# Three conversion steps of the second expert unit moved behind the third unit's rows, and a store taken out of the scatters' order

## The chip, the cores and the metric

The kernel runs on one core of a Trainium2 chip. The metric is the time of one execution on the device in microseconds (us). Five engines work side by side, each through its own queue in order: TensorE (PE, its weight loads shown apart as PEld), VectorE (DVE), ScalarE (ACT), GpSimd (POOL) and SyncE (SP), which issues nearly all transfers. They wait for one another by semaphores.

## The reference

Three layers follow one another: attention, a mixture of experts with one expert for each token, and a dense pair of layers with an ELU between them.

```python
scores_l = scale * q @ k.T ; scores_l where |pos_i - pos_j| < 16 else -1e9
scores_s = scale * q @ max_of_32(k).T + log(32)
a = softmax(concat(scores_l, scores_s)) ; x = a @ concat(v, mean_of_32(v))
...
expert_idx = argmax(x @ w_gate) ; gate_w = its softmax value      # 8 experts
disp[e, n] = x of the n-th token of expert e, up to capacity 384
y = relu(disp @ w1[e]) @ w2[e] ; out[i] = gate_w[i] * y[its place]
...
h = out @ w_in ; g = h if h > 0 else exp(h) - 1 ; result = g @ w_out
```

There are 2 x 768 = 1536 tokens of 512 values; w1 and w2 are 512x1024 and 1024x512 for each expert, w_in is 512x2048 and w_out 2048x512. w_in and w_out arrive as 64-bit floats.

## The kernel before

**First stage.** Twelve tiles of 128 tokens pass through attention and the gate. The gate of a tile (`gate_1` to `gate_4`) finds its expert and the token's place there; `put` then writes the tile's 128 rows of 514 floats to the DRAM buffer `xdisp` by an indirect transfer that POOL issues (L775). All twelve transfers belong to a group "put" whose members do not wait for one another. Behind the expert regions `xdisp` has 384 spare rows, which SP fills with a constant (`fill`, L904) in the step `n == 21`, two steps before the stage ends. The first unit's rows are read back early (`XROW0`, scaled at L267).

**Second stage.** The experts that got tokens are worked on in units of up to 384 rows, one unit behind the other, behind branches on the number of units (`units`, `unit`). With this input three units run. In each, eight tiles of hidden values are formed (`hidden`, products at L241) and used three tiles later (`second_1`, products at L275). Each float32 operand is split in a rounded part (ACT) and a remainder (DVE): the weights at L233/L234 (`split_a`, names wa..) and L286/L287 (`split_b`, names wb..), hidden values at L1270/L1271 (hh, hl), the unit's rows at L256/L257 (`split_x`, xh, xl). The rows of the third unit are split in its prologue, at the head of `unit(2)`.

**Conversions.** Beside that, DVE turns the 64-bit w_in and w_out into float32, a pair of 128-row blocks at a time, in three steps each (L419, L422, L412, tiles win and wout from raw). `ORDER` gives the sequence of the 16 pairs. The second unit does places 5 to 9 of it and the third unit places 10 to 14, spread over the hidden tiles by `convert_some`. Two raw buffers, `raw0` and `raw1`, take turns; the third step of a pair has SP load the pair after next into the buffer just freed (L378, `conv_next`).

**Third stage.** `group` works through the dense layers in groups of 384 rows (L241 again, and L1383).

Work is put on each engine in the order in which the code is written; no scheduler reorders it. In `unit`, for hidden tile `f`, that order is: finish the last unit's tile, hidden products, the split of the next weights, ReLU and split of the hidden values, `convert_some(j, f)`, `second_1(f - 3)`, `split_b`, and for the second unit at `f == 6` the split of the third unit's first weights (`prologue(2, 0)`).

Of the kernel before, what the change touches and what calls it, by code (L numbers as in the profile page):

```python
# [26 lines left out]
E, F = 8, 1024  # L27
FF = 2048
P = 128
# [9 lines left out]
REG = NT + SLOT  # L39
# [55 lines left out]
def moe_chain_kernel(  # L95
# [14 lines left out]
    nc = tc.nc  # L110
# [3 lines left out]
    xdisp = dram.tile([E * REG + SLOT, ROW], F32, name="xdisp")  # L114
# [19 lines left out]
    fill = fill_row.unsqueeze(1).to_broadcast([P, NS, ROW])  # L134
# [300 lines left out]
    with ExitStack() as att:  # L435
# [437 lines left out]
        def late(n):  # L873

            for pr, h in BMAX.get(n, ()):
                block_max(1, pr, slice(0, S) if h is None else halves[h])
            i = n // 2 + 1 if n % 2 == 0 else (n + 3) // 2
            if i < NTT:
                g = 1 - n % 2
                if n == 0 or g == 0:  # L880
                    new_kw(i)
                    put_edges(i, nc.vector)
                if i % TPB < 2 and (n == 0 or g == 0):
                    put_ks(i, dve_scaled if i >= TPB else pool_scaled)
                put_kw(i, dve_scaled, gs=(0, 1) if n == 0 else (g,))
            if n == 0:
                nc.sync.dma_start(wg[:, :, 0:E], w_gate.rearrange("p (k e) -> p k e", e=E))
                nc.sync.dma_start(cap_raw, capacity.to_broadcast([P, 1]))
                nc.vector.memset(ones_f, 1.0)
            if n == 1:  # L890
                for g in range(2):
                    put_spread(2, g, nc.gpsimd.tensor_copy)
                nc.gpsimd.memset(fill_row, 0.0)
            if n == 3:
                nc.gpsimd.tensor_copy(fill_row[:, DM:], C("oob")[:, 0:2])
                nc.gpsimd.tensor_copy(oobs, C("oob")[:, 0:1].to_broadcast([P, REG // P]))
            if n == 5:
                nc.vector.tensor_copy(tri_b, C("tri"))
                nc.vector.tensor_copy(cap, cap_raw.bitcast(I32)[:, 0:1])
            if n in (1, 3):  # L900
                load_k(1, 0 if n == 1 else 2, 2)
            if n == 21:
                nc.sync.dma_start(ids.rearrange("(p a) o -> p (a o)", a=REG // P), oobs)
                nc.sync.dma_start(xdisp[E * REG :, :].rearrange("(s p) d -> p s d", p=P), fill)  # L904
            if n == 0:
                load_q(2)
            if n % 2 == 1 and (n + 5) // 2 < NTT:
                load_q((n + 5) // 2)
            if n % 2 == 1 and (n - 1) // 2 + 2 < NTT:
                load_vx((n - 1) // 2 + 2)  # L910
            if n in VT_AT:
                load_vt(1, VT_AT.index(n))
            if n in VSUM_AT:
                pair_sum(1, VSUM_AT.index(n), nc.gpsimd, 4)
            for c, at in enumerate((14, 17)):
                hi, lo = (t.rearrange("p k n -> p (k n)") for t in WA[c])
                src = W1_RAW[c].rearrange("p k n -> p (k n)")
                if n == at:
                    nc.scalar.copy(hi, src)
                if at < n <= at + 4:  # L920
                    w = KD * 2 * P // 4
                    cols = slice((n - at - 1) * w, (n - at) * w)
                    nc.gpsimd.tensor_tensor(lo[:, cols], src[:, cols], hi[:, cols].bitcast(F32), op=ALU.subtract)
            if n in (10, 11, 12):
                m = (10, 11, 12).index(n)
                block_means(1, m, 0, m == 0, m == VC - 1)
            if n == 13:
                keep_means()
            for slot in {13: [0], 15: [1]}.get(n, ()):
                load_means(slot)  # L930
            for slot, j in MEANS_AT[1].get(n, ()):
                put_half(slot, j)
            if n == 7:
                nc.vector.tensor_scalar(e0_i, r0[0:1], -1.0, float(E), op0=ALU.mult, op1=ALU.add)
            if n == 8:
                unit_order()
            if n == W_FROM - 1:
                e0 = st["e0"] = nc.sync.value_load(e0_i, min_val=0, max_val=E - 1)
                nc.sync.dma_start(xdisp[ds(e0 * REG, SLOT), :].rearrange("(s p) d -> p s d", p=P), fill)
            if n == W_FROM + 1:  # L940
                put(0)
            if n >= W_FROM:
                load_w(st["e0"], [m for m, at in zip(W_ORDER, W_AT) if n == at])
                if n == X_AT:
                    nc.gpsimd.tensor_copy(oh32[:, 1], oh_x.unsqueeze(2).to_broadcast([P, E, NCH]))
                    rows_0.append(load_rows(XROW0, st["e0"] * REG))
            if n == NST - 2:
                scale_x(XROW0)
            if n == RING_AT:
                for m in RING[: len(RAW)]:  # L950
                    conv_load(m, rows_0)
            if n == 22:
                for m in AHEAD[:2]:
                    conv_load(m)
# [187 lines left out]
    def listed(n, j):  # L1142
        return lists_i[:, n * MAXU + j : n * MAXU + j + 1]
# [26 lines left out]
    def convert_some(j, f):  # L1170

        if j < len(CONV_UNIT):
            n = (CONVS[j + 1] - CONVS[j]) // 2
            todo = [step for m in range(n) for step in conversion(ORDER[CONVS[j] // 2 + m])]
            lo, hi = (min(m, NF1 - 1) * len(todo) // (NF1 - 1) for m in (f, f + 1))
            for step in todo[lo:hi]:
                step()

    def expert_of(j, queue=nc.sync):
        return queue.value_load(listed(0, j), min_val=0, max_val=E - 1)  # L1180
# [4 lines left out]
    def prologue(j, n):  # L1185

        if n == 0:
            split_a(0, W1_RAW[0])
        elif n == 1:
            for _ in split_x(XROW, HP[1:] + HP[:1], j % 2):  # L1190
                pass
# [56 lines left out]
    def unit(j, expert, finish):  # L1248

        if j > 1:  # L1250
            load_w(expert, NEXT[2])
            for n in range(j == 2, 2):
                prologue(j, n)
        base = nc.sync.value_load(listed(2, j), min_val=0, max_val=NT)
        if j + 1 < MAXU:
            branch_ahead(f"units{j}", n_units > j + 1)
        put_ids(j, base)
        if j + 1 < MAXU:
            load_x(j + 1)
        for f in range(NF1):  # L1260
            c, jj = divmod(f, 2)
            if f < LAG:
                finish(f)
            hp = hidden(WA[c % 2], jj, XS1)
            if jj == 0 and c + 1 < NC1:
                split_a(c + 1, W1_RAW[c + 1])
            hf = HF[f % 2]
            hh, hl = HH[f % 4]
            nc.scalar.activation(hf, hp, AF.Relu)
            nc.scalar.copy(hh, hf)  # L1270
            nc.vector.tensor_tensor(hl, hf, hh.bitcast(F32), op=ALU.subtract)  # L1271
            convert_some(j, f)
            if f >= LAG:
                second_1(f - LAG)
            if jj == 0:
                split_b(WB[c % 2], W2_RAW[c])
            if j == 1 and f == NF1 - 2:
                prologue(2, 0)
            if j > 1 and f == Y_AT:
                load_y(0, 0)  # L1280
            if j > 1 and f == NF1 - 1:
                start_second()
            if f in ROWS_AT and j + 1 < MAXU:
                scale_x(XROW, [ROWS_AT.index(f)])
            if f in NEXT_AT and j + 1 < MAXU:
                n = NEXT_AT.index(f)
                if n == 0:
                    expert = expert_of(j + 1)

                any_next = nc.values_load(listed(NLIST - 1, 0), engines=[nc.sync.engine], min_val=0, max_val=MAXU)  # L1290
                with tc.If(any_next > j + 1):
                    load_w(expert, NEXT[n])

        def rest(n):
            second_1(NF1 - LAG + n)
            if n == LAG - 1:
                evict(base)

        return expert, rest
# [12 lines left out]
    def units(j, expert, finish):  # L1312
        if j:
            expert, finish = unit(j, expert, finish)
        if j + 1 < MAXU:
            with tc.If(n_units > j + 1, label=f"units{j}") as more:
                units(j + 1, expert, finish)
            with more.Else():
                if j:
                    last_parts()  # L1320
                if j + 1 < len(CONV_UNIT):
                    for n in range(CONVS[j + 1], NCHUNK - CONV_LATE, 2):
                        convert(ORDER[n // 2])
        else:
            last_parts()
# [228 lines left out]
```

## Time and profile before

| what | value |
|---|---|
| median of three runs | 422.8 us (420.69 to 423.19) |
| the profiled execution | 421.81 us |
| its span, first to last instruction | 419.7 us |
| PE busy | 398.4 us (95%) |
| DVE busy | 336.1 us (80%) |
| ACT, POOL busy | 234.7 us, 64.8 us |
| mean granted PE clock | 0.993 of full |

The span is what the trace covers; 2.1 us of the profiled execution lie around it. PE's busy share counts matmuls whose ends are modelled, so small waits between them matter more than the share suggests. A granted clock of 1.00 is 2.4 GHz, one of 0.50 is 1.2 GHz. Times in the trace count from the span's start: the first stage ends near 105 us, the second unit lies at 135 to 165 us, the third at 165 to 210 us, the third stage behind it.

### The profile page before, as it was taken

The page shows a single profiled execution, that of the slowest core. Times are in us where ns is not written, and L with a number is a line of the kernel's source. Part 1 is how long each engine was busy: PE and PEld are TensorE (multiplying, and loading weights), DVE is VectorE, ACT ScalarE, POOL GpSimd, SP SyncE. Part 2 cuts the span into 40 slices and gives each one's busy share as a digit, 9 for nine tenths or more (in the row PEclk, how much of TensorE's full clock was granted, in tenths as well). Part 3 has the DMA queues.
Part 4 walks back from the last instruction along what each step waited for, and adds up shares of the span by engine and source line. Part 5 has one row for each costly group of instructions (what it writes and reads, how often), then busy time and mean ns, then how long its engine had stood idle before and what let it go on. Part 6 is the DMA issues. An engine that isn't in the chain of part 4 may idle for free.

```text
span 419.7 us, 7891 instructions
## 1 busy us (share of the span) xinstructions
PE 398.4 (95%) x2736; PEld 349.1 (83%) x2736; DVE 336.1 (80%) x675; ACT 234.7 (56%) x586; POOL 64.8 (15%) x129
## 2 busy tenths in 40 slices
PE   7999999989999999799999999999999999999994
PEld 4577677667898989799989889998989898989883
DVE  6789787686589988788879999997788777778870
ACT  4687697762565737166497578645343435343421
POOL 5334776515300000000000000002000002000002
PEclk9999999999999999899999999999999999999998
DMA  8999999699476786985577000202000200100002
GB/s 245 256 285 263 270 275 280 188 345 364 155 228 226 244 301 232 332 255 209 171 271 274 0 2 1 77 0 77 0 0 2 76 2 35 40 2 0 2 2 77
DMA packets 33691, 63.60 MB, mean 152 GB/s; under 512 B 5302, under 2 KB 16191, under 8 KB 33642
## 3 DMA queue, kind: packets, MB, share of 16 engines
q1 hardware_dynamic: 31962, 58.28, 44.9%
q0 software_dynamic: 1680, 4.73, 3.1%
q8 instruction: 23, 0.38, 0.4%
q14 instruction: 26, 0.21, 0.1%
HBM read 50.19 MB, written 13.40 MB: 152 GB/s over the span
## 4 chain that ended last, share of the span: by engine, by line
PE 48%; issue 19%; DVE 16%; DMA 7%; ACT 6%; POOL 1%; SPq 1%; DVEq 0%; another core or an unknown queue 0%; ACTq 0%; POOLq 0%
PE bank L241 21%; PE bank L1383 13%; PE bank L275 5%; DMA half<-in_q_dram 3%; PE bank L661 2%; PE bank L615 2%; ACT ex L640 2%; DMA w2raw<-in_v_dram 2%; PE bank L675 2%; DMA rows<-in_k_dram 2%; DMA raw<-in_moe_w_out_dram 1%; DVE wal L234 1%; DVE win L422 1%; DVE win L412 1%; DVE xrow L1445 1%
## 5 line engine op out<-in xcount | busy, mean ns | idle before, releaser
L1383 PE MATMUL bank<-wout_r,hh 128*128 128x512 f32 x144 | 56.6, 393 | 1.0 <-DVE wout_r L1363 1.0
L640 ACT ACTIVATE ex<-bank,nm 128x120 f32<-128x120 f32 x96 | 33.5, 370 | 9.9 <-DVE nm L627 9.9
L1430 ACT ACTIVATE cst<-bank 128x384 f32<-128x384 f32 x24 | 11.8, 490 | 39.2 <-PE bank L241 39.2
L1430 ACT ACTIVATE xrow<-bank 128x384 f32<-128x384 f32 x24 | 11.7, 489 | 38.4 <-PE bank L241 38.2
L1383 PEld LDWEIGHTS bank<-wout_r,hh 128*128 128x128 f32 x144 | 27.1, 188 | 5.9 <-DVE wout_r L1363 1.7
L1395 POOL DMA_INDIRECT out_dram<-ysb,idt x3 | 2.9, 973 | 178.8 <-DVE xrow L1446 178.2
L1383 PE MATMUL bank<-w2raw_r,hl 128*128 128x512 f32 x72 | 28.7, 399 | 0.5 <-DVE hl L1411 0.5
L1383 PE MATMUL bank<-w2raw_r,hh 128*128 128x512 f32 x72 | 28.2, 392 | 0.0
L241 PE MATMUL bank<-yh,win_r 128*128 128x384 f32 x128 | 27.0, 338 | 0.0
L615 PE MATMUL bank<-kw,half 128*64 128x120 f32 x384 | 24.7, 271 | 1.4 <-DMA half<-in_q_dram 1.4
L1395 POOL DMA_INDIRECT out_dram<-raw,idt x6 | 6.1, 1024 | 119.3 <-ACT raw L1392 118.1
L615 PEld LDWEIGHTS bank<-kw,half 128*64 128x64 f32 x384 | 19.7, 136 | 5.7 <-issue 5.1
L241 PE MATMUL bank<-xh,wal 128*128 128x384 f32 x104 | 23.4, 347 | 0.6 <-DVE wal L234 0.6
L241 PEld LDWEIGHTS bank<-yh,win_r 128*128 128x128 f32 x128 | 22.8, 188 | 0.3
L275 PE MATMUL bank<-hh,wbh_r 128*128 128x384 f32 x96 | 21.1, 341 | 0.0
L1445 DVE SCALAR_TENSOR_TENSOR xrow<-xrow 128x384 f32<-128x384 f32 x24 | 13.3, 556 | 9.2 <-ACT xrow L1432 8.5
L640 ACT ACTIVATION_READ_ACCUMULATOR ex<-bank,nm 128x1 f32 x96 | 20.6, 215 | 0.0
L275 PE MATMUL bank<-hl,wbh_r 128*128 128x384 f32 x96 | 20.6, 336 | 0.0
L1445 DVE SCALAR_TENSOR_TENSOR xrow<-cst,xrow 128x384 f32<-128x384 f32 x24 | 13.3, 556 | 8.6 <-ACT cst L1432 8.6
L241 PEld LDWEIGHTS bank<-xh,wal 128*128 128x128 f32 x104 | 18.7, 193 | 1.8 <-DVE wal L234 1.6
L661 PE MATMUL bank<-cst,ex 128*120 128x128 f32 x96 | 17.2, 289 | 0.7 <-ACT ex L640 0.5
L666 ACT COPY es<-bank 120x512 f32<-120x512 f32 x24 | 14.2, 593 | 6.3 <-PE bank L661 4.4
(286 smaller groups left out, 1108.0 us busy)
## 6 DMA issues: line engine op xcount, KB each, us to landing
raw<-in_moe_w_out_dram SPq DMA_DIRECT2D x16, 512.0 KB
w1raw<-in_moe_w_dram SPq DMA_DIRECT2D x12, 512.0 KB
w2raw<-in_moe_w_dram SPq DMA_DIRECT2D x12, 512.0 KB
raw<-in_moe_w_in_dram SPq DMA_DIRECT2D x10, 512.0 KB
half<-in_q_dram SPq DMA_DIRECT2D x24, 128.0 KB
w2raw<-in_v_dram SPq DMA_DIRECT2D x6, 512.0 KB
rows<-in_moe_w_in_dram SPq DMA_DIRECT2D x6, 512.0 KB
yr<-ydT SPq DMA_DIRECT2D x4, 768.0 KB
```

Of the source, the lines that this page charges most:

```text
L234: nc.vector.tensor_tensor(lo, src, hi.bitcast(F32), op=ALU.subtract)
L241: nc.tensor.matmul(hp, wa[a][:, kk, cols], xa[b][:, kk, :], start=(n == kk == 0), stop=(n == 2 and kk == KD - 1))
L275: nc.tensor.matmul(ACC[d][:, 0:SLOT], wb[a][:, jj, d * P : (d + 1) * P], hb[b], start=(f == 0 and n == 0), stop=(f == NF1 - 1 and n == 2),)
L615: nc.tensor.matmul(sp[cols, u, :], qts[i][:, g, u, cols], kws[i][:, g, u, j, :], start=True, stop=True)
L640: nc.scalar.activation(ex[:, u, :], sp[:, u, :], AF.Exp, bias=nm[:, u : u + 1], accum_out=dens[i][:, g, u])
L661: nc.tensor.transpose(ep[:, u, :], ex[:, u, :], ident)
L666: nc.scalar.copy(es, st.pop(("e", i, g)))
L675: nc.tensor.matmul(op[j * TQ : (j + 1) * TQ, u, :], es[:, u, j * TQ : (j + 1) * TQ], vx[:, j, (2 * u + g) * D : (2 * u + g + 1) * D], star ...
L1383: nc.tensor.matmul(ACC[s], ga[a][:, cols], wb[b][:, jj, :], start=(f == n == 0), stop=(f == NF2 - 1 and n == 2),)
L1395: put = nc.gpsimd.indirect_dma_start(out, bass.IndirectOffsetOnAxis(ap=IDT[g % 3][:, s : s + 1], axis=0), OBS[(NS * g + s) % len(OBS)], No ...
L1430: nc.scalar.activation(x, hp, AF.Relu, scale=-1.0)
L1445: nc.vector.scalar_tensor_tensor(z, x, 1.0, z, op0=ALU.add, op1=ALU.mult)
```

## The change

There are two edits. First, the store to the spare rows joins the group "put": neither it nor the scatters wait for one another, and the reads of `xdisp` that follow wait for it as they do for the scatters. Second, the last three DVE steps of the second unit (the conversion of place 9 in `ORDER`, tile wout_108 from raw0) are not issued at `f == 6` but kept in a list. They are issued in the third unit behind its prologue, so behind the split of its rows, and with them goes the load that follows the third step. Where there is no third unit, the same steps stand at the head of the other branch.

```diff
-                nc.sync.dma_start(xdisp[E * REG :, :].rearrange("(s p) d -> p s d", p=P), fill)
+                spare = nc.sync.dma_start(xdisp[E * REG :, :].rearrange("(s p) d -> p s d", p=P), fill).ins
+                tc.declare_no_dep(spare, group="put", reason="no token has a row there")
+                tc.add_to_no_dep_group("put", spare)
+                puts.append(spare)
...
-            for step in todo[lo:hi]:
-                step()
+            if j == 1 and f == NF1 - 2:
+                put_off.extend(todo[lo:])
+            elif j != 1 or not put_off:
+                for step in todo[lo:hi]:
+                    step()
+
+    put_off = []
+
+    def convert_rest():
+        for step in put_off:
+            step()
...
             for n in range(j == 2, 2):
                 prologue(j, n)
+            if j == 2:
+                convert_rest()
...
             with more.Else():
+                if j == 1:
+                    convert_rest()
                 if j:
                     last_parts()
```

On POOL, at the end of the first stage, the eighth scatter stands behind the row and index computations of its tile; the names in brackets are the semaphores that an instruction waits for, where DMAHW5 is raised by the spare rows' store. One piece of the difference:

```order
-L763 TENSOR_TENSOR row<-row,rank 128x1 [waits Pool_49]
-L764 TENSOR_SCALAR idx<-row,ob 128x1 [waits Pool_49]
-L775 DMA xdisp<-xr,idx 15744x514 [waits DMAHW2_49,DMAHW3_49,DMAHW1_49,DMAHW5_49,Activation_49,Pool_49]
...
+L763 TENSOR_TENSOR row<-row,rank 128x1 [waits Pool_49]
+L764 TENSOR_SCALAR idx<-row,ob 128x1 [waits Pool_49]
+L775 DMA xdisp<-xr,idx 15744x514 [waits DMAHW2_49,DMAHW1_49,DMAHW3_49,Activation_49,Pool_49]
```

Nothing moved on POOL; the wait for DMAHW5 is gone, and those for DMAHW1 to 3, which the three reads of the first unit's rows raise, stay.

On DVE, from the last hidden values but one of the second unit to the first weights of the third (hl and hh are parts of hidden values, wbl_r and wal parts of weights, xl the remainders of the third unit's rows), before:

```order
L1271 TENSOR_TENSOR hl_156<-cst,hh_155 128x384
L419 TENSOR_SCALAR wout_108<-raw_160 128x1024
L422 SCALAR_TENSOR_TENSOR wout_108<-raw_160,wout_108 128x1024
L412 SCALAR_TENSOR_TENSOR wout_108<-raw_160,wout_108 128x1024
L287 TENSOR_TENSOR wbl_r<-w2raw_137,wbh_r 128x1024
L234 TENSOR_TENSOR wal_141<-w1raw_123,wah_r 128x1024
L1271 TENSOR_TENSOR hl_1901<-cst,hh_1900 128x384
...
L257 TENSOR_TENSOR xl_93<-bank_84,xh_92 128x384
...
L257 TENSOR_TENSOR xl_93<-bank_91,xh_92 128x384
...
L234 TENSOR_TENSOR wal_143<-w1raw_125,wah_142 128x1024
```

The same stretch of DVE with the change:

```order
L1285 TENSOR_TENSOR hl_156<-cst,hh_155 128x384
L287 TENSOR_TENSOR wbl_r<-w2raw_137,wbh_r 128x1024
L234 TENSOR_TENSOR wal_141<-w1raw_123,wah_r 128x1024
L1285 TENSOR_TENSOR hl_1901<-cst,hh_1900 128x384
...
L257 TENSOR_TENSOR xl_93<-bank_84,xh_92 128x384
...
L257 TENSOR_TENSOR xl_93<-bank_91,xh_92 128x384
L419 TENSOR_SCALAR wout_108<-raw_160 128x1024
L422 SCALAR_TENSOR_TENSOR wout_108<-raw_160,wout_108 128x1024
L412 SCALAR_TENSOR_TENSOR wout_108<-raw_160,wout_108 128x1024
...
L234 TENSOR_TENSOR wal_143<-w1raw_125,wah_142 128x1024
```

The three steps went past two weight splits, one split of hidden values and the four splits of the third unit's rows, and stand ahead of the unit's second weights. On SP the load into raw0 that follows the third step went past the five loads of the third unit's weights that stood behind it.

## Rows read from the trace of the kernel before

**Rows 1.** Windows of 2 us: busy time by engine, clock, DMA share, GB/s

```profile
88.00:90.00 2.00, 1.30 (x11) 1.15 (x11) 1.11 (x7) 1.19 (x7) 0.00 (x0) 1.00 1.05 367
172.00:174.00 2.00, 2.00 (x8) 2.00 (x7) 1.23 (x2) 0.00 (x0) 0.00 (x0) 0.50 1.04 354
```

**Rows 2.** Timeline, end of the first stage: start, length, instruction, [idle before <- releaser]

```profile
86.87 0.61 SPq L904 DMA_DIRECT2D xdisp<-fill_row  x1
...
97.76 1.10 POOL L775 DMA_INDIRECT xdisp<-xr,idx  x1 [12.43 <-ACT wbl L705]
...
83.97 1.28 DVE L267 TENSOR_SCALAR rows<-rows,gate 128x512 f32<-128x512 f32 x3
...
92.60 0.69 DVE L419 TENSOR_SCALAR win<-raw 128x1024 uint32<-128x1024 uint32 x1
```

**Rows 3.** Timeline, last gates and the unit lists, DVE, PE and POOL

```profile
99.37 0.16 DVE L732 TENSOR_REDUCE r<-vv 128x1 f32<-128x8 f32 x1 [1.76 <-POOL row L757]
...
99.86 0.18 PE L750 MATMUL bank<-oh,tri_b 128*128 128x8 bf16 x1 [0.89 <-DVE oh L734]
...
108.55 0.18 POOL L1088 MEMSET prod<- 32x72 f32 x1
...
108.76 0.15 DVE L1096 TENSOR_TENSOR prod<-am,cst 32x2 f32<-32x2 f32 x1 [0.98 <-issue]
...
109.69 0.28 PE L1107 MATMUL bank<-prod,ones_f 32*1 32x72 f32 x2 [0.84 <-DVE prod L1101]
```

**Rows 4.** Timeline of DVE, from the second unit into the third

```profile
162.29 0.55 DVE L1271 TENSOR_TENSOR hl<-cst,hh 128x384 fp32r<-128x384 f32 x1
164.28 0.69 DVE L419 TENSOR_SCALAR wout<-raw 128x1024 uint32<-128x1024 uint32 x1 [1.44 <-DMA raw<-in_moe_w_out_dram]
165.01 1.23 DVE L422 SCALAR_TENSOR_TENSOR wout<-raw,wout 128x1024 uint32<-128x1024 uint32 x1
166.27 1.23 DVE L412 SCALAR_TENSOR_TENSOR wout<-raw,wout 128x1024 uint32<-128x1024 uint32 x1
167.41 1.22 DVE L287 TENSOR_TENSOR wbl_r<-w2raw,wbh_r 128x1024 fp32r<-128x1024 f32 x1
...
170.15 1.94 DVE L257 TENSOR_TENSOR xl<-bank,xh 128x384 fp32r<-128x384 f32 x4
172.01 1.22 DVE L234 TENSOR_TENSOR wal<-w1raw,wah 128x1024 fp32r<-128x1024 f32 x1
```

**Rows 5.** Timeline of PE's weight loads, same stretch

```profile
167.12 0.71 PEld L275 LDWEIGHTS bank<-hl,wbh_r 128*128 128x128 f32 x4
...
170.76 0.65 PEld L241 LDWEIGHTS bank<-xh,wah_r 128*128 128x128 f32 x4 [2.92 <-DVE xl L257]
171.39 1.25 PEld L241 LDWEIGHTS bank<-xh,wal 128*128 128x128 f32 x4
...
175.04 0.71 PEld L275 LDWEIGHTS bank<-hh,wbl_r 128*128 128x128 f32 x4
```

**Rows 6.** Timeline of ACT, same stretch

```profile
160.05 1.06 ACT L286 CAST wbh_r<-w2raw 128x1024 fp32r<-128x1024 f32 x1 [0.16 <-PE bank L275]
161.00 1.05 ACT L233 CAST wah_r<-w1raw 128x1024 fp32r<-128x1024 f32 x1
...
165.01 1.66 ACT L256 CAST xh<-bank 128x384 fp32r<-128x384 f32 x4 [0.22 <-PE bank L255]
```

**Rows 7.** Timeline of SP, DVE and PE's weight loads: raw loads and their users

```profile
157.79 0.83 SPq L378 DMA_DIRECT2D raw<-in_moe_w_out_dram  x2
...
181.55 0.69 DVE L419 TENSOR_SCALAR wout<-raw 128x1024 uint32<-128x1024 uint32 x1
183.06 1.23 DVE L234 TENSOR_TENSOR wal<-w1raw,wah_r 128x1024 fp32r<-128x1024 f32 x1 [0.82 <-ACT wah_r L233]
...
187.56 0.71 PEld L241 LDWEIGHTS bank<-xh,wal 128*128 128x128 f32 x4
...
212.30 1.22 DVE L1363 TENSOR_TENSOR win_r<-win,wah 128x1024 fp32r<-128x1024 f32 x1 [4.00 <-ACT wah L1362]
```

## The prediction

> **What bounds the kernel now.** I first read the page's busy shares and clock: PE is busy for 95% of the span, so a change gains only where PE stands still or runs slowly, and such places have to be found one by one. I then read the list of waits, longest first, for the two stretches that the diff touches, and last the timelines of PE and of the engine that each of its waits names. The reader is to see two things.
>
> At the end of the first stage POOL stands still for 12.43 us before the eighth scatter [rows 2]. The row names an ACT instruction as releaser, but the scatter needs nothing from it; the order of the change shows which wait is dropped, that for the spare rows' store, issued at 86.87. POOL had been free since 97.76 - 12.43 = 85.33. What stands behind that scatter on POOL comes late in turn: DVE waits 1.76 us for it and PE then 0.89; a clearing of `prod` (108.55) keeps DVE waiting for 0.98 and PE for 0.84 [rows 3].
>
> Between the second and the third unit PE loads no weights for 2.92 us, until the first `xl` has been written [rows 5]. DVE is what it waits for: it took up the last conversion late, at 164.28, since its raw data had just landed, and the weight splits and the four `xl` come behind [rows 4]. Behind this pause PE runs at half clock: 0.50 granted, which is 1.2 GHz, in 172 to 174 [rows 1].
>
> **The moved conversion, part by part.** Without the three steps DVE goes from the hidden remainder (done at 162.29 + 0.55 = 162.84) straight to the weight splits. ACT's halves of these are done at 161.11 and 162.05 [rows 6], so nothing holds them. From the start of `wbl_r` to that of the first `xl` took 170.15 - 167.41 = 2.74 us [rows 4]; from 162.84 that gives 165.6. ACT's four copies of the rows begin at 165.01 and take 1.66 [rows 6], so the first is there by 165.4. The first `xl` ends near 166.1 and all four, 1.94 us, near 167.6. PE's previous loads end at 167.12 + 0.71 = 167.83 [rows 5]. So PE goes on at 167.83 instead of 170.76 with 1.7 us to spare, and the 2.92 us go whole.
>
> The slow clock is the second term. From 170.76 to 175.04 four groups of four weight loads take 4.28 us; at full clock a group takes 0.70 (0.71 in the rows at either end, which overlap a little), so 2.8 [rows 5]. The clock fell after the pause and there is no pause now, so I take the 1.5 us as regained; the other end is nothing. Together 2.92 + 1.5 = 4.4, bounds 2.9 and 4.4.
>
> What is added: the three steps, 0.69 + 1.23 + 1.23, with their overlaps 3.1 us, now at 167.6 to 170.7. Next on DVE are the unit's second weights, which ran at 172.01 [rows 4] and now start at 170.7, before they did. So the displaced work costs nobody anything. DVE also entered the third stage with 4.00 us of idle time, waiting for ACT [rows 7]; the pushed work is not carried into that stage.
>
> The third step also issues a load on SP. It stood behind the step's end at 167.5 and now comes at about 170.8, behind five weight loads that waited for it before and now go out earlier, which costs nothing. Its user is the step at 181.55 [rows 7]; with PE 4.4 us earlier DVE gets there at 177.1 at the earliest, 6.3 us after the issue. The last such load took from 157.79 to 164.21, 6.4 us [rows 7, 4]. So DVE may wait a little there, 0 to some tenths. PE does not feel it: it wants the `wal` that follows on DVE at 187.56 - 4.4 = 183.1 [rows 7], and the step and that split take 0.69 + 1.23 = 1.9, so the load may take until 181.2, 10.4 us. I take 0.
>
> **The store, part by part.** Nothing is added on any queue: SP issues the same store at the same place. The scatter keeps its wait for the three reads of the first unit's rows, but these rows were scaled by DVE at 83.97 [rows 2], so they had landed. It goes out at about 85.4, and the POOL work behind it no longer waits. PE's 0.89 go, since DVE's 1.76 are more than that. PE's 0.84 go as well: the clearing of `prod` stands behind the last scatters in POOL's queue, which now come when their indices are ready, and DVE's 0.98 cover the 0.84 [rows 3]. Sum 0.89 + 0.84 = 1.7. From above, DVE's two waits bound it, 1.76 + 0.98 = 2.7, if DVE rather than PE leads there; from below 0, or a loss if the scatters get in the way of loads. I take 1.7, PE's own rows. The gain is handed on: behind 110 us the lists, the branches and the second unit's loads all hang on this chain.
>
> The scatters now fall into a stretch in which the DMA engines have nothing to spare: share 1.05 at 367 GB/s in 88 to 90 [rows 1]. The Trainium skill speaks against this edit here (DMA: Bandwidth & Descriptors, section "Issuing engines are not separate DMA queues"): transfers started by SP and by GpSimd run on the same 16 engines and interleave, so an earlier scatter takes its time from SP's loads. The share of 1.05 fits that; with the rule alone the 1.7 could be lost whole. Three scatters of 128 x 514 x 4 bytes, 0.79 MB, come forward past such loads; at 367 GB/s this is 2.2 us. The first user is the conversion step at 92.60, which waited for nothing [rows 2]; I take it as covered.
>
> **Sum.** The profiled execution took 421.81. 421.81 - 4.4 - 1.7 = 415.7. It lies 1.0 below the median of the three runs; the mean of all four times is 422.1, so I add 0.3: **416.0 us**.
>
> **The rivals.** *Loads pay for the early scatters.* The conversion at 92.60 waits up to 2.2 us, and the attention's last rows stand behind it on DVE. The gain at 99.86 and 109.69 is then used up: 416.0 + 1.7 = 417.7. For it speaks the full DMA share; against it that the raw load is issued ahead of the scatters and was not waited for. Chance 0.12.
>
> *The clock falls all the same.* If PE's clock at 171 to 175 hangs on something else than the pause, or another short pause takes its place, 1.5 us stay: 417.5. Against it: the fall comes right behind the pause, and the weight load at 167.12, ahead of it, took the same 0.71 as at full clock. Chance 0.08.
>
> *The change does little of what it says.* DVE stays PE's releaser between the units, for instance because a weight split waits on PE for its buffer (ACT waited for PE until 160.05 [rows 6]), and half of the 4.4 goes too: 419 to 421. Chance 0.07.
>
> *Slower than before: the postponed load starves the raw buffers.* Each later load of the third unit hangs on a conversion that waits for an earlier one, twice in a row for each buffer. If a load takes L, PE loses about 2 x (L - 10.4), and each such pause brings the slow clock again, 2 x 1.5. That eats the 6.1 us from L = 12 on; at L = 13 the kernel would take 416.0 + 2 x 2.6 + 3 = 424. Against it: 6.4 us measured, and 10.9 even for the spare rows' store under full load (86.87 to 97.76 [rows 2]). Chance 0.03.
>
> **How the numbers follow.** Forecast 0.70, rivals 0.12, 0.08, 0.07 and 0.03. One per cent, 4.2 us, is about what a measurement of this kernel can tell from no change. The forecast lies 6.1 to 6.8 below; the first two rivals lie near the bound, 4.4 to 5.1 below, and are split, two thirds to faster. So faster 0.70 x 0.97 + 0.67 x 0.20 = 0.81, less a little for what I have not seen: 0.78; same 0.19; slower 0.03. The range goes down to both upper bounds, 422.1 - 4.4 - 2.7 = 415.0, less 1.2 for the scatter of the runs: 413.8. Upward it takes in the first two rivals, 417.7, and the same scatter: 419.0.
>
> **What would show it.** The eighth scatter near 85.5; no wait of PE before L750 and the product with `prod`; in the third unit `xl` ahead of the conversion, no PE pause before its first hidden products, the clock at 1.00 there. Wrong would be a DVE wait for raw data at the first conversion or in the third unit followed by one of PE, a clock of 0.50 in a new place, or DVE without idle time at the entry to the third stage.

## The result, and the profile after

The changed kernel takes 417.88 us in the median of six runs (416.39 to 419.24), beside 422.51 for the kernel before. The ratio is 0.9898 with a 95% interval of 0.9868 to 0.9927, so 4.6 us are gained where 6.1 to 6.8 were forecast. The profiled execution took 419.24 (span 417.4, clock 0.992), the slowest of the six.

The windows of 2 us of the changed kernel come first (columns as in [rows 1]). In the first the DMA engines are still as good as full, with share 1.00. The second is the stretch in which the clock had been 0.50; it is 1.00 now.

```profile
88.00:90.00 2.00, 0.88 (x6) 0.47 (x5) 1.23 (x6) 1.79 (x10) 0.73 (x4) 1.00 1.00 344
...
172.00:174.00 2.00, 2.00 (x13) 2.00 (x12) 1.97 (x3) 0.29 (x1) 0.00 (x0) 1.00 1.03 366
```

At the end of the first stage the timeline of the changed kernel reads as follows, to be held against [rows 2, 3]. This run comes to this place 1.16 us later than the run before, so 92.60 answers to 93.76.

```profile
84.20 0.44 SPq L904 DMA_DIRECT2D xdisp<-fill_row  x1
...
86.77 1.10 POOL L775 DMA_INDIRECT xdisp<-xr,idx  x1 [0.28 <-POOL idx L764]
...
93.76 0.69 DVE L419 TENSOR_SCALAR win<-raw 128x1024 uint32<-128x1024 uint32 x1
...
100.06 0.18 PE L750 MATMUL bank<-oh,tri_b 128*128 128x8 bf16 x1
...
107.77 0.15 POOL L1091 MEMSET prod<- 32x72 f32 x1
...
108.98 0.28 PE L1110 MATMUL bank<-prod,ones_f 32*1 32x72 f32 x2
```

The eighth scatter waits for 0.28 us, not 12.43, the clearing of `prod` comes ahead of its user, and PE waits at neither product. The conversion at 93.76 waits for nothing.

Between the second and the third unit the changed kernel's DVE and PE's weight loads stand as follows, against [rows 4, 5].

```profile
162.05 1.22 DVE L287 TENSOR_TENSOR wbl_r<-w2raw,wbh_r 128x1024 fp32r<-128x1024 f32 x1
...
164.80 1.95 DVE L257 TENSOR_TENSOR xl<-bank,xh 128x384 fp32r<-128x384 f32 x4
166.67 0.68 DVE L419 TENSOR_SCALAR wout<-raw 128x1024 uint32<-128x1024 uint32 x1
...
166.40 0.71 PEld L275 LDWEIGHTS bank<-hl,wbh_r 128*128 128x128 f32 x4
167.10 0.71 PEld L241 LDWEIGHTS bank<-xh,wah_r 128*128 128x128 f32 x4
...
169.87 0.71 PEld L275 LDWEIGHTS bank<-hh,wbl_r 128*128 128x128 f32 x4
```

The `xl` stand ahead of the conversion and PE goes on without a pause. The group that began at 175.04 begins at 169.87. Ahead of the boundary the two runs were 0.72 apart, so 4.45 us were gained here.

Up to 178 us the changed kernel is 5.2 us ahead, yet its span is only 2.3 shorter. Its timeline from 165 us on shows where the rest went (SP, DVE, ACT, PE's weight loads):

```profile
165.28 4.72 SPq L201 DMA_DIRECT2D w2raw<-in_moe_w_dram  x2
171.15 1.59 SPq L378 DMA_DIRECT2D raw<-in_moe_w_out_dram  x2
173.83 0.33 SPq L1195 DMA_DIRECT2D ids<-it  x1
...
178.35 0.84 SPq L378 DMA_DIRECT2D raw<-in_moe_w_out_dram  x2
...
177.58 0.69 DVE L419 TENSOR_SCALAR wout<-raw 128x1024 uint32<-128x1024 uint32 x1 [1.11 <-DMA raw<-in_moe_w_out_dram]
...
186.32 0.69 DVE L419 TENSOR_SCALAR wout<-raw 128x1024 uint32<-128x1024 uint32 x1 [2.45 <-DMA raw<-in_moe_w_out_dram]
...
188.60 0.73 ACT L269 ACTIVATE xrow<-xrow,gate 128x512 f32<-128x512 f32 x1 [7.58 <-DVE gate L264]
...
190.32 0.65 PEld L241 LDWEIGHTS bank<-xh,wah 128*128 128x128 f32 x4 [0.29 <-ACT wah L233]
191.58 0.65 PEld L241 LDWEIGHTS bank<-xh,wal 128*128 128x128 f32 x4 [0.61 <-DVE wal L234]
...
202.82 0.64 PEld L275 LDWEIGHTS bank<-hh,wbl_r 128*128 128x128 f32 x4 [0.84 <-DVE wbl_r L287]
...
208.23 0.65 PEld L241 LDWEIGHTS bank<-yh,wal 128*128 128x128 f32 x4 [1.24 <-DVEq L1514]
```

The first raw load of these rows, at 171.15, is the postponed one. It stands in SP's row behind the weight loads and waits there for earlier landings, as SP's list of waits for 145 to 215 us says (total, times, longest):

```profile
SPq L378 <- DMA w1raw<-in_moe_w_dram: 1.9, 2, 1.1
```

It holds up all that follows: the ids, the next unit's rows (176.67), and only then, at 178.35, the next raw load. The buffer of that load had been free since the end of this step, 175.25 + 1.22 = 176.47, so the load went out 1.9 us later than it could:

```profile
175.25 1.22 DVE L412 SCALAR_TENSOR_TENSOR wout<-raw,wout 128x1024 uint32<-128x1024 uint32 x1
```

DVE waits 2.45 us for that data. Behind DVE's wait stand the gate of the rows, behind that ACT's `xrow` and `wah`, and behind these PE, which waits four times, 0.29 + 0.61 + 0.84 + 1.24 = 2.98 us.

### The profile page after: what moved, and what is told of

It reads as the page before. It is cut to its first block, busy times and chain, and to the rows that moved or that the text cites. A ratio compares the mean times of both kernels' runs of the same rounds, so it can differ in the third digit from the quotient of the medians.

```text
span 417.4 us, 7892 instructions
## 1 busy us (share of the span) xinstructions
PE 399.0 (96%) x2736; PEld 348.6 (84%) x2736; DVE 335.7 (80%) x675; ACT 234.9 (56%) x586; POOL 65.5 (16%) x129
## 5 line engine op out<-in xcount | busy, mean ns | idle before, releaser
L627 DVE TENSOR_REDUCE nm<-bank 128x4 f32<-128x480 f32 x24 | 15.6, 650 | 3.7 <-PE bank L615 3.3
```

The source lines that it names most:

```text
L627: nc.vector.tensor_reduce(nm, sp, axis=AX.X, op=ALU.max, negate=True)
```

## The experiments

To compare runs whose first stages differ I measure three stretches between the same work, by the starts of PE's weight loads. These are the four rows in the changed kernel: a product with `tri_b` at the end of the first stage, the product with `prod`, the first transposes of the third unit, and the first wait for `wout_r` in the third stage.

```profile
89.86 0.10 PEld L482 LDWEIGHTS <-tri_b 128*128 128x128 bf16 x1 [1.29 <-issue]
...
108.97 0.08 PEld L1110 LDWEIGHTS bank<-prod,ones_f 32*1 32x1 f32 x2 [0.25 <-issue]
...
163.39 0.09 PEld L250 LDWEIGHTS bank<-cst,xrow 128*3 128x3 f32 x2 [0.25 <-issue]
...
217.33 0.19 PEld L1399 LDWEIGHTS bank<-wout_r,hh 128*128 128x128 f32 x1 [1.34 <-DVE wout_r L1379]
```

S is the stretch from the first to the second (the store's), U from the third to the fourth (the third unit). From the second to the third every kernel takes 54.4 to 54.5 us, and from the fourth to the end 199.7 to 200.1. So a profiled run differs from another in S, in U and in when it reaches the first row, which ranges from 86.8 to 91.5 and shows no trend with the edits (89.0 on the mean with the store's edit, 89.2 without).

| kernel | first row | S | U | median us | ratio to before, 95% interval |
|---|---|---|---|---|---|
| before | 88.70 | 20.96 | 55.58 | 421.4 to 422.5 | |
| changed | 89.86 | 19.11 | 53.94 | 417.88 | 0.9898 [0.9868, 0.9927] |
| e1 store alone | 90.85 | 19.12 | 56.52 | 420.54 | 0.9975 [0.9948, 1.0001] |
| e9 store alone, again | 88.47 | 19.12 | 56.93 | 420.44 | 0.9963 [0.9936, 0.9990] |
| e2 steps alone | 90.88 | 20.00 | 53.60 | 419.26 | 0.9951 [0.9917, 0.9985] |
| e3 load late | 88.36 | 20.88 | 55.51 | 421.37 | 1.0006 [0.9975, 1.0037] |
| e4 both, load on POOL | 89.77 | 19.10 | 51.76 | 416.64 | 0.9893 [0.9859, 0.9926] |
| e5 changed, again | 88.53 | 19.12 | 55.01 | 417.36 | 0.9896 [0.9853, 0.9939] |
| e6 both, load on POOL | 87.56 | 19.11 | 52.44 | 414.79 | 0.9841 [0.9804, 0.9878] |
| e7 both, load on ACT | 87.62 | 19.12 | 52.50 | 415.71 | 0.9865 [0.9827, 0.9903] |
| e8 both, rows first | 86.77 | 19.11 | 57.04 | 419.52 | 0.9970 [0.9928, 1.0013] |
| e10 steps, load on POOL | 88.95 | 19.12 | 51.88 | 417.23 | 0.9898 [0.9864, 0.9931] |
| e11 both, load on POOL | 91.47 | 19.12 | 51.28 | 416.22 | 0.9876 [0.9844, 0.9908] |

e1 to e4, e5 to e8 and e9 to e11 ran each on one chip beside the kernel before, with medians of 421.38, 421.40 and 422.03.

U can be taken apart. Adding up PE's weight loads' waits of over 0.27 us in it (2.92 in the kernel before, 2.98 in the changed one) and taking them off leaves 52.6 to 52.7 in the four kernels whose steps stand in the old place (before, e1, e3, e9) and 50.9 to 51.3 in the nine with the moved steps. Each of the four has a granted clock of 0.50 in 172 to 174, and none of the nine has less than 1.00 there; the 1.3 to 1.8 us between the groups fit the 1.5 that was forecast for the slow clock. So PE's waits and this stretch are all in which U differs.

**The theory.** Both edits pay what was forecast where they stand. The postponed load then makes SP's row late, and the third unit gives part back. **Rivals:** one edit brought all of it; the DMA engines, not SP's row, are the limit; the loss is that one run's.

**e1 and e9: the store's edit alone.**

```diff
-                nc.sync.dma_start(xdisp[E * REG :, :]...
+                spare = nc.sync.dma_start(xdisp[E * REG :, :]...
+                tc.declare_no_dep(spare, group="put", ...
+                tc.add_to_no_dep_group("put", spare)
+                puts.append(spare)
```

> The kernel before with the store's edit alone. Theory T (both edits pay what was forecast where they stand, 1.7 to 1.9 us for the store and 4.4 us for the moved steps, and the third unit gives 1.6 to 2.9 us back because the postponed raw load comes late in SP's row): 1.8 us faster than before, about 420.7 us; PE's waits of 0.89 and 0.84 us at 100 to 110 us gone, nothing else changed. Rival R1 (the moved steps brought the whole of the 4.6 us and the store nothing): 422.5 us.

> The store's edit alone once more, since the first measurement, 0.25% faster with an interval from 0.52% faster to nothing, does not settle it. Theory T, with what the traces now show (PE comes from the softmax of the last tiles to the product with prod 0.9 to 1.85 us sooner, the less the later the first stage runs): 0.9 to 1.8 us faster than before. Rival R5 (the store's wait costs nothing as a rule): no difference.

Measured 0.25% and 0.37% faster; the first interval just takes in no change, the second does not. S is 19.12 in both, 1.84 under the kernel before, as forecast. But U is 0.9 and 1.35 us longer than before, which no theory had. Rows of e9, DVE and PE's weight loads:

```profile
162.94 0.69 DVE L419 TENSOR_SCALAR wout<-raw 128x1024 uint32<-128x1024 uint32 x1 [2.20 <-DMA raw<-in_moe_w_out_dram]
...
169.42 0.65 PEld L241 LDWEIGHTS bank<-xh,wah_r 128*128 128x128 f32 x4 [3.69 <-DVE xl L257]
```

The last conversion of the second unit, still in its old place here, waits 2.20 us for its data (1.44 in [rows 4]), and PE's pause behind it is 3.69 (2.92 in [rows 5]). The load took 7.2 us from its issue at 155.70 to its use, and 7.1 in e1, against 6.5 in the kernel before and 6.4 in e3. In e9 the pause is thus 0.77 longer and PE waits another 0.63 at 209.84 (0.61 and 0.39 in e1), which is what U lost to within 0.1. Part of the store's gain is handed back, mostly at the pause that the other edit removes. Whether the load is slower because of the store's edit, two runs against two do not settle.

**e2: the moved conversion alone.**

```diff
+            if j == 1 and f == NF1 - 2:
+                put_off.extend(todo[lo:])
...
             for n in range(j == 2, 2):
                 prologue(j, n)
+            if j == 2:
+                convert_rest()
```

> The kernel before with the moved conversion alone. Theory T: 4.4 us at 167 to 171 us, less 1.6 to 2.9 us in the third unit, 419.6 to 421.0 us; DVE waits for raw data in the third unit (1.1 us, then about 2.5 us) and PE then waits some 2 to 3 us in all between about 190 and 210 us. Rival R1: 417.9 us, with no such waits of PE, those of the profiled run after being that run's own.

Measured 0.49% faster, 2.1 us. U is 53.60, and PE waits 0.38 + 0.61 + 0.52 + 1.11 = 2.62 us between 192 and 210. So the loss in the third unit belongs to the moved conversion and to more than one run, and the rival that it brought the whole gain falls. S is 20.00 without the store's edit: this run came 2.2 us later to its first row than the run before, the store went out at 87.02 as there (86.87), and its wait cost 0.88 us instead of 1.85.

**e3: the load's place alone.** The steps stay; the load goes where the change puts it. While `waiting` holds a list, the third step puts its load there instead of issuing it.

```diff
+            nonlocal waiting
+            if j == 1 and f == NF1 - 2:
+                waiting = behind
             for step in todo[lo:hi]:
                 step()
+            waiting = None
...
+    def load_late():
+        for i in behind:
+            conv_load(i)
...
             for n in range(j == 2, 2):
                 prologue(j, n)
+            if j == 2:
+                load_late()
```

> The kernel before, its steps where they were, but the raw load that the last conversion of the second unit sets free is issued where the changed kernel issues it, behind the third unit's prologue and so behind five weight loads in SP's row and ahead of the ids. Theory T: the load's place by itself costs the third unit what it cost there, 1.6 to 3 us, so 424.1 to 425.5 us, with DVE waiting for raw data twice and PE some 2 to 3 us between 190 and 215 us. Rival R2 (the DMA engines are short of time there because everything comes 5 us sooner, and the place in the row does not matter): 422.5 us.

Measured no difference (1.0006), so the theory as I had put it falls: the place by itself costs nothing. Rows of e3, SP and DVE:

```profile
171.48 1.69 SPq L378 DMA_DIRECT2D raw<-in_moe_w_out_dram  x2
174.22 0.33 SPq L1193 DMA_DIRECT2D ids<-it  x1
...
181.14 0.82 SPq L378 DMA_DIRECT2D raw<-in_moe_w_out_dram  x2
...
188.15 0.69 DVE L419 TENSOR_SCALAR wout<-raw 128x1024 uint32<-128x1024 uint32 x1
```

SP's row runs at nearly the same times as in the changed kernel (171.15, 173.83), for the five weight loads no longer wait behind the raw load and go out 5.1 to 5.6 us earlier than before. In e3 the next raw load then waits for DVE to free its buffer and goes out at 181.14. In the kernel before, the ids and this load stood here:

```profile
176.68 0.34 SPq L1183 DMA_DIRECT2D ids<-it  x1
...
181.66 0.82 SPq L378 DMA_DIRECT2D raw<-in_moe_w_out_dram  x2
```

The row is late only for a DVE that is 5 us ahead. So the theory is now: the steps came forward by 5.2 us in the profiled runs, the ids behind them on SP by 2.85 (176.68 to 173.83), and the difference is what DVE and PE wait for.

**e4, e6 and e11: the postponed load on POOL**, which has nothing else to do there.

```diff
-    def conv_load(i, after=()):
+    def conv_load(i, after=(), queue=nc.sync):
...
-            ld = nc.sync.dma_start(raw_pair(i)...
+            ld = queue.dma_start(raw_pair(i)...
...
     def convert_rest():
+        nonlocal waiting
+        waiting = []
         for step in put_off:
             step()
+        for i in waiting:
+            conv_load(i, queue=nc.gpsimd)
+        waiting = None
```

> The changed kernel, with the postponed raw load (two transfers of 512 KB) issued by POOL, which has nothing else to do there, so that SP's row goes from the weight loads straight to the ids and the next unit's rows. Theory T: those go out 2.6 us sooner, the following raw load 1.9 us sooner, and PE's waits of 3.0 us in the third unit shrink to under 1 us: 415 to 416.3 us. Rival R2 (the DMA engines are the limit, not SP's row): 417.9 us, the same waits.

> The postponed load on POOL, beside the changed kernel on the same chip. Theory T by the first traces: from the third unit's transposes to the first product that waits for wout 51.8 us against 53.9, so 1.5 to 2.2 us faster than the changed kernel. Rival R2 (what the trace shows there is paid back or was that one run's): the same time.

> Both edits with the load on POOL, beside the two runs above on the same chip. Theory T: the sum of the two, 4 to 5.6 us faster than before, near 416 us where before has 421.4; the two measurements so far gave 4.5 and 6.7 us. Rival R6 (the two gains overlap): no better than the moved conversion alone with the load on POOL.

Rows of e6: POOL, SP, DVE and PE's weight loads.

```profile
167.87 1.16 POOL L378 DMA_DIRECT2D raw<-in_moe_w_out_dram  x2 [62.25 <-DVE wout L412]
...
168.09 0.34 SPq L1200 DMA_DIRECT2D ids<-it  x1
...
174.19 0.82 SPq L378 DMA_DIRECT2D raw<-in_moe_w_out_dram  x2
...
172.95 1.22 DVE L412 SCALAR_TENSOR_TENSOR wout<-raw,wout 128x1024 uint32<-128x1024 uint32 x1
...
175.95 0.70 DVE L419 TENSOR_SCALAR wout<-raw 128x1024 uint32<-128x1024 uint32 x1 [1.78 <-DMA raw<-in_moe_w_out_dram]
...
182.70 0.69 DVE L419 TENSOR_SCALAR wout<-raw 128x1024 uint32<-128x1024 uint32 x1 [0.45 <-DMA raw<-in_moe_w_out_dram]
...
204.42 0.65 PEld L241 LDWEIGHTS bank<-yh,wal 128*128 128x128 f32 x4 [1.01 <-DVEq L1519]
```

The ids go out right behind the weight loads, 7.0 us behind the first transposes (161.09) against 10.4 in the changed kernel. The second DVE wait shrinks from 2.45 to 0.45, and PE's waits to 1.4 us (0.7 in e4, none in e11). U is 51.28 to 52.44 in the three, against 53.60 to 55.01 with the load on SP.

The next raw load shows that SP's row was the limit. Here its buffer is free at 172.95 + 1.22 = 174.17 and it goes out at 174.19. It follows that end by at most 0.03 us in every run with the postponed load off SP (e4, e6, e7, e10, e11), and in the kernel before and e3; with the steps moved and the load on SP ahead of the rows it is 1.9, 1.7 (e2) and 2.6 us late (e5). What is left of DVE's waits for raw data in the three, 1.18 to 2.23 us, is the loads' own time, most of it that of the postponed load; that much of the rival stays.

On time, e6 is 2.6 us under the changed kernel on the same chip, more than was expected. The first measurement, e4, showed nothing of it against the first of the changed kernel (0.9893 and 0.9898; 416.64 where 416.3 at most was expected), and e11 lies between. The mean of the three ratios is 0.9870, against 0.9897 for the two with the load on SP. So the stretch is shown shorter in all traces, and the time likely by a little over one us; the intervals overlap.

The load itself is not quicker on POOL: issue to use took 8.1 us in e6 and 7.7 in e4, against 6.4 from SP in the changed kernel. That is the sense of the Trainium skill (DMA: Bandwidth & Descriptors, section "Issuing engines are not separate DMA queues"): transfers interleave on the same engines whoever starts them, and another issuer saves only the time that the sequencer takes to initiate a transfer, usually little beside the transfer itself. The traces agree: the load is no quicker, and its two issues took SP only 0.35 us each in the changed kernel. What was saved here is something else, the 1.9 us for which SP's row stood still for landings while the row loads waited behind it.

**e7 and e8: is it POOL, or the freed row?** e5 is the changed kernel beside them, with no edit. e7 differs from the version on POOL in one word:

```diff
-            conv_load(i, queue=nc.gpsimd)
+            conv_load(i, queue=nc.scalar)
```

e8 keeps the load on SP and issues it behind the ids and the rows:

```diff
     def convert_rest():
+        nonlocal waiting
+        waiting = behind
         for step in put_off:
             step()
+        waiting = None
+
+    def load_behind():
+        for i in behind:
+            conv_load(i)
...
         if j + 1 < MAXU:
             load_x(j + 1)
+        if j == 2:
+            load_behind()
```

> The changed kernel once more, beside the three that follow, so that they are compared on one chip. Every theory: about 1.0% under before. Its trace, theory T: SP's ids for the third unit at about 173.8 us and the raw load behind the rows at 178.4, as in the first profile, a DVE wait of about 2.5 us on that load, and 3 us of PE's waits between 190 and 210 us.

> The postponed load issued by ACT behind the third unit's splits. Theory T (it matters only that SP's row is freed of it): as fast as with POOL to within half a us, since ACT has 2.65 us of idle time there and waits for DVE till about 169.8 us; SP's ids at about 170.8 us. Rival R3 (POOL's own queue is what helps, by another way into the DMA engines): the same time as the changed kernel or slower.

> The changed kernel with the postponed load on SP, but behind the ids and the three row loads of the next unit instead of ahead of them. Theory T (SP's row can serve only one of the two in time): ids at about 170.8 us, rows from 173.7 us, the postponed load at about 175.4 us, its data at 182 us where DVE asks at 176.5 us; DVE waits 5 to 6 us there and the third unit loses 3 us or more against the changed kernel: about 421 us where that has 418. Rival R4 (the rows' place alone cost the 3 us): as fast as with POOL.

e5 shows the first profile's loss again and larger: ids at 173.24, DVE waits of 1.75 and 3.26, PE's waits 1.72 + 0.61 + 0.62 + 1.12 = 4.07. e7 is 1.65 us faster than e5 (and 0.9 slower than e6, a little more than expected), and its U is that of POOL, so it is the freed row and not POOL's own way to the DMA engines. In e8 the ids go out at 168.54, yet it is 2.2 us slower than e5, where 3 or more were expected. Timeline rows of SP (the postponed load and, from 174.09, the next), DVE and PE, then three windows of 2 us:

```profile
173.14 1.79 SPq L378 DMA_DIRECT2D raw<-in_moe_w_out_dram  x4
...
180.54 0.69 DVE L419 TENSOR_SCALAR wout<-raw 128x1024 uint32<-128x1024 uint32 x1 [7.17 <-DMA raw<-in_moe_w_out_dram]
...
182.43 0.79 PE L241 MATMUL bank<-xh,wal 128*128 128x384 f32 x3 [2.79 <-DVE wal L234]
```

```profile
180.00:182.00 2.00, 0.00 (x0) 0.00 (x0) 1.46 (x2) 0.00 (x0) 0.00 (x0) 1.00 0.95 302
182.00:184.00 2.00, 1.57 (x9) 1.57 (x10) 1.97 (x3) 0.00 (x0) 0.00 (x0) 1.00 1.01 383
184.00:186.00 2.00, 2.00 (x13) 2.00 (x12) 1.99 (x2) 0.00 (x0) 0.00 (x0) 1.00 0.18 65
```

DVE waits 7.17 us for the postponed load and PE 2.8 behind it. PE's four later waits, 0.73 + 0.62 + 0.58 + 1.08 = 3.0 us, stand where the changed kernel has its own, though DVE waits for no further raw data: being late from the first wait is enough. So the rows' place alone is not the cost either. With both on SP, one or the other comes late; moving the load off the row serves both.

**e10: the moved conversion with the load on POOL, without the store's edit**, which is taken out of e4:

```diff
-                spare = nc.sync.dma_start(xdisp[E * REG :, :]...
-                tc.declare_no_dep(spare, group="put", ...
-                tc.add_to_no_dep_group("put", spare)
-                puts.append(spare)
+                nc.sync.dma_start(xdisp[E * REG :, :]...
```

> The moved conversion without the store's edit, and the postponed load on POOL. Theory T: the term of 4.4 us comes through nearly whole once SP's row is free of the load, less PE's waits of 0.7 to 1.4 us that are left, so 3 to 3.8 us faster than before, against the 2.1 us that the moved conversion brought by itself with the load on SP. Rival R2: 2.1 us again.

Measured 1.02% faster, 4.3 us, and more than was expected; U is 51.88, 3.7 under before. That is twice e2; the profiles put 1.7 us of the difference in U and 0.9 in S, where neither edits anything. Its S is 19.12 although the scatter still waits for the store:

```profile
95.33 1.09 POOL L775 DMA_INDIRECT xdisp<-xr,idx  x1 [9.75 <-DMA xdisp<-fill_row]
```

Here SP issued the store at 83.35, 3.5 us earlier than in [rows 2] and 5.6 ahead of the row that opens S (1.8 in the kernel before). POOL stood still for 9.75 us and PE for none of it. Beside it on the same chip e11, which adds the store's edit, is 1.0 us faster (416.22), with intervals that overlap; so what that edit adds here on time is not settled.

## Why the prediction came out as it did

The range held the time and the sign was right; the forecast was 1.9 us too low, and the gain, 1.0%, lies on the bound that I had set between faster and the same. That the time lies so near 417.7 and 417.5, which two of the rivals gave, is luck: neither of the two came about, and the loss that took their place was priced at 0. Two of the signs of being wrong that I had named did come, a DVE wait for raw data in the third unit followed by one of PE, and a clock of 0.50 in a new place.

- *PE's pause, 2.92, and the slow clock, 1.5.* Right in place: 4.45 measured against 4.4, by the same steps. The rival that the clock falls all the same did not come about: it is 1.00 in 172 to 174. The 1.5 is borne out by U less PE's waits, above. The profiled run did have 0.50 from 76 to 78, in the first stage, before anything that the change moves. e4 and e10 have it there too and e2 from 40 to 42; e5 to e8 and e11 have no such stretch, nor have the four kernels with the pause. What it has to do with the change, if anything, stays open.
- *"I take 0" for the postponed load.* This is the step that failed. I asked only whether DVE and PE could bear that load's own lateness, and gave it 10.4 us. Its own wait was 1.11 us, more than the some tenths forecast, and PE did not feel it (in e11, a wait of 1.18 there is followed by none of PE). But behind the load on SP stood the ids, the next unit's rows and the next raw load, and I priced none of them, although the code puts them there, behind `convert_rest`. They cost PE 2.98 us in the profiled run, 2.62 in e2 and 4.07 in e5. With SP freed the conversion edit brings 3.1 to 4.3 us in U (51.28 to 52.44 against 55.58), up to nearly the 4.4.
- *The starved raw buffers.* The rival had the right place and the wrong condition. It wanted loads of 12 us; in the profiled run the loads took 6.4 and 8.0 from issue to use, and the second was issued late. (The load that I gave 6.4 us took 6.5 to its use, 157.79 to 164.28 by [rows 4, 7]; nothing hangs on it.)
- *The store, 0.89 + 0.84 = 1.7.* Right in the profiled run: 1.85. I took it as fixed, however, and it is not. Over the four runs with the wait it cost 1.85, 1.76 (e3), 0.88 (e2) and 0 (e10), the less the earlier the store goes out against the first stage's own progress. So the term is rather 1.1 on the mean of these four. Over all thirteen runs the store went out 1.75 to 5.66 us ahead of the row that opens S, 3.8 on the mean, which is e2's place; by that, an estimate, it is about 0.9. Its two measurements alone, 0.25% and 0.37%, fit that or the gain handed back in U; they cannot tell which.
- *The early scatters.* They cost no load that DVE waited for: the conversion at 93.76 has no wait. The rule of the Trainium skill that spoke against the edit (DMA: Bandwidth & Descriptors, the same section as above) took nothing away here that these runs could measure.

The profiled pair adds up: 1.85 in S and 1.64 in U were gained, 1.16 was lost by the later first stage, and 417.4 stands against 419.7. The 1.16 is no cost of the edits' waits but fits that run's slow stretch in 76 to 78: e9 starts the product ahead of it at 74.35 as well, has no such stretch, and reaches the first row 1.39 us sooner (88.47 against 89.86). The medians differ by 4.6, and by 4.0 for e5, which is 1.1 and 1.6 us more than S and U of these two profiles give; e4 and e10 gain 0.7 to 0.9 less than theirs give. A first stage that ranges over 4.7 us from run to run can hold such differences, but no run shows that it does.

## What to carry to other kernels

When a step is moved, follow every DMA that it issues into its queue and price what stands behind it there, not only the user of its own data: in the profiled run the load itself cost PE nothing and its followers cost 3 us. When a pause of the bound engine is removed, ask which loads were issued in time only because of that pause, for they do not come forward with the work. If an engine with nothing else to issue there can start the transfer, its waits hold up nothing behind it, though the transfer itself is no quicker.

## What the runs showed of the hardware

PE's clock does not fall after every pause of the same length. In [rows 5] a pause of 2.92 of the weight loads (2.61 of the products) was followed by 0.50 in 172 to 174, and so were pauses of the products of 2.50 (e3), 3.21 (e1) and 3.37 (e9) at the same place. In e8 one of 2.79 of the products, with no PE work at all in 180 to 182, was followed by 1.00 in every window. In the changed kernel's first stage a pause of 1.16 us before the product at 74.35 was followed by 0.50 from 76 to 78; in e1 and e9, before the same product, one of 1.19 was followed by 1.00. The rows of the changed kernel and then of e9, PE's product and a window of 2 us:

```profile
74.35 1.35 PE L661 MATMUL bank<-cst,ex 128*120 128x128 f32 x4 [1.16 <-ACT ex L640]
76.00:78.00 2.00, 2.00 (x24) 1.64 (x20) 1.66 (x4) 1.40 (x7) 1.21 (x3) 0.50 0.29 46
...
74.35 1.35 PE L661 MATMUL bank<-cst,ex 128*120 128x128 f32 x4 [1.19 <-ACT ex L640]
76.00:78.00 2.00, 2.00 (x40) 1.76 (x36) 1.63 (x4) 1.43 (x7) 1.18 (x3) 1.00 0.32 85
```

From that product to the first row of the table the changed kernel, e4 and e10, all with the stretch of 0.50, take 15.5 us, e1 and e9 14.1: the slow clock alone costs 1.4 us there. What decides whether the clock falls these runs do not show. The 1.5 us that I counted as regained came back in all nine kernels without the pause, but a pause does not always cost them.
